# The last 128 output rows in 64-row product tiles, and a second program of products, evacuations and transfers appended to the kernel

## The chip, the core and the metric

The kernel runs on one core of a Trainium2 chip. The metric is device time in microseconds from the launch to the end of the program on that core; lower is better. One core has a matrix engine (PE, with its weight loads PEld), a vector engine (DVE), an activation engine (ACT), a general engine (POOL), a queue engine for transfers (SP) and 16 DMA engines. PE reads its operands from SBUF and writes to PSUM, which has 8 banks of 128 partitions by 512 float32.

## What is computed

A transformer layer with two parallel branches on a normalized input: attention with 32 query heads that share one key and one value head, and a two-layer network with squared ReLU.

```
xn = layernorm(x)                                  # x: 1 x 2048 x 640, bfloat16
q  = (xn @ wq) as 32 heads of 20;  k = xn @ wk;  v = xn @ wv
p  = softmax(q k^T * 20**-0.5) ;   o = p v
A  = o (heads joined, 640) @ wo
h  = relu(xn @ w1 + b1)**2                          # 1536 wide
B  = h @ w2 + b2
out = x + A + B                                     # 2048 x 640
```

## The kernel before

The sequence is cut into 4 column blocks of 512 queries and 16 tiles of 128 keys, and the 32 heads into 8 groups of 4, so that there are 32 blocks (query block, head group). For each block and key tile, PE makes the scores of four heads as four products that each use 20 to 32 rows of the array, one 32-row group per head (line 1014, and line 1231 for the other way below), ACT takes the exponential out of two or three PSUM banks at a time (line 1056), and PE multiplies by the values with four 32-column tiles of the array, one per head, into one bank, `PVB` (bank 7). A part of the score tiles goes another way: DVE writes an integer approximation of the exponential (line 1245), POOL makes further terms by integer additions (line 1265), and some terms are summed by accumulating transfers that POOL issues, 512 KB each (line 1280). The projections, the network and the output products run between the attention steps, again as four 32-column tiles per step (`col4`, line 426 is the one line that issues them, in `mm`).

No engine's order is written by hand. A planner in the kernel's own Python keeps a clock per engine, gives each operation a modelled duration, and repeatedly commits the operation that can start first; the order in which they were committed is the order in which each engine executes. [...]

**The end of the program.** The output of the last 512 rows is made in eight halves (`halves`: four row tiles, 12 to 15, of 128 rows, by two halves of 320 columns). Each half is a sum of six products: four blocks of attention output with `wo_c`, and two with `woe`, a padded copy of the last eight heads' rows of `wo` that is kept in the storage of `w1_sb` (so the profile calls it `w_sb`, and its left operand `QCr`). One product is four matmuls of 128 rows by 32 columns with 320 moving columns, one per 32 output rows. `tail_ops` (from line 1307) offers these products to the planner as banks come free, and `tail_done` (from line 1330) queues the evacuation of a finished half, a DVE addition of the network's part from `part` (line 1346), and after each second half the output transfer of that row tile (line 830, `odma`). The sixth product of every half needs the last head group's normalized output (`TB31`, a DVE transpose, line 1122). At the end SP waits for the output transfers' semaphores (line 1638).

Of the kernel before, what the change touches and what calls it, by code (L numbers as in the profile page):

```python
# [24 lines left out]
NCH = D // 128  # L25
NXR, NFP, NOS = 3, 4, 3
HW = D // 2
SCALE = DH ** -0.5
EPS = 1e-5
EXP_SHIFT = 50.0  # L30
# [14 lines left out]
XA = SCALE * LOG2E * 128.0  # L45
XB = (127.0 - EXP_SHIFT * LOG2E - math.log2(TNORM)) * 128.0

PTR = 16
NB = 7
# [155 lines left out]
def add(lst, fn, waits=(), inc=None, amt=1):  # L205
    wd = {}
    for c, v in waits:
        if v is None or v <= 0:
            continue
        key = id(c)  # L210
        if key not in wd or wd[key][1] < v:
            wd[key] = (c.sem, v)
    w = list(wd.values())
    tgt = None
    sem = None
    if inc is not None:
# [12 lines left out]

    lst.append(emit)  # L230
    return tgt


class Op:
    def __init__(self, name, eng, dur, parts, deps=(), lat=None, lock=False, mode="C", prio=3, dma=None):
        self.name, self.eng, self.dur, self.parts = name, eng, dur, parts
        self.deps = [d for d in deps if d is not None]
        self.lat, self.lock, self.mode, self.prio = lat, lock, mode, prio
        self.dma = dma
        self.start = self.fin = None  # L240
# [8 lines left out]
        self.dw = 0.0  # L249
        if dma is not None:  # L250
            dma.n += 16
            self.tgt = (dma, dma.n)
# [10 lines left out]
def bass_parallel_sum__grouped_kv_mqa__dense_activation_squared_relu__prompt_kernel(nc, A_x, A_wq, A_wk, A_wv, A_wo, B_x, B_w1, B_b1, B_w2, B_b2, out):  # L263
    es = ExitStack()
    with es:
# [3 lines left out]
        def newctr(name):  # L269
            return Ctr(es.enter_context(nc.semaphore(name)))  # L270
# [154 lines left out]
        def mm(out_, l, r, start, stop, tp):  # L425
            return lambda e: e.matmul(out_, l, r, start=start, stop=stop, tile_position=tp)  # L426
# [880 lines left out]
        def tail_ops():  # L1307

            r = []
            for x in halves:  # L1310
                if x["c"] < NCH:
                    bk = x["bank"] if x["bank"] is not None else tail_bank()
                    if bk is None:
                        break
                    t_ = tb_op.get((qe, x["c"]))
                    if t_ is None or t_.fin is None:
                        continue
                    r.append((x, bk, 2.5))
                    break
            for x in halves:  # L1320
                if x["c"] == NCH and (qe, NCH) in tb_op:
                    r.append((x, x["bank"], 1.9))
                    break
            for x, bk, p in r:
                c, st, h = x["c"], x["st"], x["h"]
                mats, cs = out_mats(st, h, [c], False)
                deps = [tb_op[(qe, c)]] + (l_woe[c - NCH + 1] if c >= NCH - 1 else l_wo) + ([bank_rel[bk]] if c == 0 else [])
                yield Op(f"OF{st}_{h}_{c}", "PE", 0.136, out_chunks(mats, bk, c == 0, c == NCH)[0][1](), deps), p, x, bk

        def tail_done(o, x, bk):  # L1330
            st, h = x["st"], x["h"]
            if x["c"] == 0:
                x["bank"] = bk
                bank_busy[bk] = True
            x["c"] += 1
            if x["c"] <= NCH:
                return
            cs = slice(h * HW, h * HW + HW)
            free_row = tn_op[NBLK - 1] if st == ST - 1 else dma_out.get(st - NOS)
            k = 2 * (st - 4 * qe) + h  # L1340
            if k in ACTEV:
                i = ACTEV.index(k)
                e_ = op(f"OFa{st}_{h}", "ACT", 0.40, lambda e: e.activation(out=xr[:, i, :], in_=ps[:, bk, 0:HW], func=AF.Identity), [o] + [fp_ev[n] for n in XORD[-NXR:]])
                f_ = op(f"OFe{st}_{h}", "POOL", 0.85, lambda e: e.tensor_tensor(out=orow(st)[:, cs], in0=xr[:, i, :], in1=part[:, st % 4, cs], op=ALU.add), [e_, fr_op[k], free_row])
            else:
                f_ = e_ = op(f"OFe{st}_{h}", "DVE", 0.40, lambda e: e.tensor_tensor(out=orow(st)[:, cs], in0=ps[:, bk, 0:HW], in1=part[:, st % 4, cs], op=ALU.add), [o, fr_op[k], free_row], prio=0.1)  # L1346
# [258 lines left out]

        for o in order_all:
            for d in o.deps:
                if not (o.eng == "PE" and d.eng == "PE"):
                    d.consumed = True

        clock = {k: {} for k in ENG}
# [1 line left out]
        for o in order_all:  # L1613
            ck = clock[o.eng]
            waits = []
            for d in o.deps:
                if o.eng == "PE" and d.eng == "PE":
                    continue
                c, v = d.tgt
                if ck.get(id(c), 0) >= v:  # L1620
                    continue
                waits.append((c, v))
                for i_, v_ in d.clock.items():
                    ck[i_] = max(ck.get(i_, 0), v_)
                ck[id(c)] = v
            o.clock = dict(ck)
            for k, fn in enumerate(o.parts):
                w = waits if k == 0 else ()
                if o.dma is not None:
                    add(lists[o.eng], lambda e, fn=fn, c=o.dma: fn(e).then_inc(c.sem, 16), waits=w)  # L1630
                elif k == len(o.parts) - 1 and o.consumed:
                    v = add(lists[o.eng], fn, waits=w, inc=eng_ctr[o.eng])
                    o.tgt = (eng_ctr[o.eng], v)
                    o.clock[id(eng_ctr[o.eng])] = v
                else:
                    add(lists[o.eng], fn, waits=w)
        for slot in range(NOS):
            add(lists["SP"], None, waits=[(osem[slot], osem[slot].n)])

# [54 lines left out]
```

## Time and profile before

| What | Value |
|---|---|
| Time, median of 2 runs | 676.42 us (675.42 to 677.43) |
| Span of the profiled execution | 688.3 us |
| Busy in that span: PE, DVE, ACT, POOL | 679.9, 607.2, 657.7, 586.2 us |
| Granted PE clock, mean | 0.973 of full speed |
| Last exponential (ACT) begins, ends | 678.29, 679.41 us |
| Last evacuation (DVE) ends | 686.1 us |
| Issue of the last output transfer | 686.12 us |

The profile shows one execution with the hardware profiler on. No device time of its own is recorded for that execution, only the span from its first to its last instruction; it is 11.9 us longer than the median of the two timed runs. Times in the views are counted from the start of the span. In the timeline, a row is a group of like instructions merged; its second number is the time from the start of its first to the end of its last. [...] The number in brackets is the idle time of the engine before the row, and who ended it.

### The profile page before, as it was taken

The page shows a single profiled execution, that of the slowest core. Times are in us where ns is not written, and L with a number is a line of the kernel's source. Part 1 is how long each engine was busy: PE and PEld are TensorE (multiplying, and loading weights), DVE is VectorE, ACT ScalarE, POOL GpSimd, SP SyncE. Part 2 cuts the span into 40 slices and gives each one's busy share as a digit, 9 for nine tenths or more (in the row PEclk, how much of TensorE's full clock was granted, in tenths as well). Part 3 has the DMA queues.
Part 4 walks back from the last instruction along what each step waited for, and adds up shares of the span by engine and source line. Part 5 has one row for each costly group of instructions (what it writes and reads, how often), then busy time and mean ns, then how long its engine had stood idle before and what let it go on. Part 6 is the DMA issues. An engine that isn't in the chain of part 4 may idle for free.

```text
span 688.3 us, 22356 instructions
## 1 busy us (share of the span) xinstructions
PE 679.9 (99%) x9554; PEld 212.3 (31%) x9555; DVE 607.2 (88%) x1081; ACT 657.7 (96%) x721; POOL 586.2 (85%) x597
## 2 busy tenths in 40 slices
PE   8999999999999999999999999999999999999998
PEld 4233222232322222333332222333332222233334
DVE  8558999899999899889998999889888999999893
ACT  6668999999999999999999999999999999999994
POOL 0406989889999999989999989999989998989982
PEclk9559999999999999999999999999999999999999
DMA  8355677767877697768977667677777765788873
GB/s 215 89 130 145 130 158 149 152 138 156 168 166 143 124 176 136 155 133 179 200 140 154 134 131 136 135 150 147 141 160 152 141 124 115 152 180 185 169 158 97
DMA packets 62894, 102.21 MB, mean 148 GB/s; under 512 B 22418, under 2 KB 40722, under 8 KB 62794
## 3 DMA queue, kind: packets, MB, share of 16 engines
q0 software_dynamic: 19296, 70.26, 54.8%
q1 hardware_dynamic: 41898, 30.14, 16.6%
q8 instruction: 75, 1.23, 0.7%
q10 hardware_dynamic: 1600, 0.38, 0.3%
q14 instruction: 25, 0.20, 0.1%
HBM read 17.71 MB, written 4.42 MB: 32 GB/s over the span
## 4 chain that ended last, share of the span: by engine, by line
PE 74%; ACT 15%; POOL 5%; DVE 3%; DMA 2%; issue 1%; DVEq 0%; POOLq 0%
PE ps L426 71%; ACT PT L1056 15%; POOL x_sb L1265 2%; DVE tmore L1245 2%; POOL tmore L1265 2%; PE ps L619 1%; DMA x_sb<-x_sb 1%; DMA tmore<-tmore 1%; PE ps L648 1%; POOL x_sb L1280 1%; DVE big L775 0%; DVE xr L823 0%; DVE out_sb L1346 0%; PE ps L581 0%; PE ps L576 0%
## 5 line engine op out<-in xcount | busy, mean ns | idle before, releaser
L1056 ACT ACTIVATE PT<-ps 128x1024 bf16<-128x1024 f32 (+2 forms) x697 | 644.7, 1107 | 16.1 <-PE ps L426 15.5
L1245 DVE TENSOR_SCALAR tmore<-ps 128x512 uint16<-128x512 f32 x644 | 417.9, 682 | 43.9 <-PE ps L426 37.9
L1265 POOL INT64_ADD tmore<-tmore x226 | 258.8, 1306 | 35.9 <-DVE tmore L1245 25.9
L426 PE MATMUL ps<-qT,kT 20*128 20x512 bf16 x2048 | 277.1, 390 | 1.2 <-ACT PT L1056 0.8
L1265 POOL INT64_ADD x_sb<-tmore x222 | 255.8, 1287 | 21.4 <-PE ps L426 4.7
L426 PEld LDWEIGHTS ps<-qT,kT 20*128 20x128 bf16 x2048 | 68.8, 91 | 265.0 <-ACT PT L1056 218.4
L426 PE MATMUL ps<-PT,vx 128*32 128x512 bf16 x1396 | 139.5, 395 | 0.1
L426 PE MATMUL ps<-xnT,w_sb 128*32 128x512 bf16 x960 | 79.3, 383 | 0.4 <-DVE tmore L1245 0.4
L426 PE MATMUL ps<-w_sb,big 128*32 128x320 bf16 x1536 | 79.2, 301 | 0.3
L1280 POOL DMA_DIRECT2D tmore<-tmore x65 | 71.2, 1112 | 2.5 <-POOL tmore L1265 2.4
L1280 POOL DMA_DIRECT2D x_sb<-tmore x65 | 67.7, 1048 | 4.8 <-POOL x_sb L1265 3.3
L426 PE MATMUL ps<-tmore,vxs 128*32 128x512 bf16 x640 | 58.3, 382 | 0.3 <-POOL tmore L1265 0.3
L426 PE MATMUL ps<-x_sb,vxs 128*32 128x512 bf16 x624 | 57.6, 383 | 0.2 <-DMA x_sb<-x_sb 0.2
L426 PEld LDWEIGHTS ps<-PT,vx 128*32 128x32 bf16 x1396 | 35.2, 93 | 73.1 <-issue 67.5
L426 PE MATMUL ps<-tmore,vx 128*32 128x512 bf16 x456 | 43.3, 382 | 0.4 <-DMA tmore<-tmore 0.4
L426 PEld LDWEIGHTS ps<-w_sb,big 128*32 128x32 bf16 x1536 | 34.3, 96 | 28.4 <-issue 16.8
L767 DVE TENSOR_SCALAR hT_tmp<-ps,b1col 128x512 bf16<-128x512 f32 x48 | 35.5, 740 | 0.9 <-PE ps L426 0.6
L426 PE MATMUL ps<-xnT,wq_sb 128*32 128x512 bf16 (+2 forms) x480 | 35.8, 366 | 0.2 <-ACT PT L1056 0.2
L426 PE MATMUL ps<-wo_c,OC 128*32 128x320 bf16 x608 | 31.6, 301 | 0.0
L426 PE MATMUL ps<-x_sb,vx 128*32 128x512 bf16 x320 | 31.3, 382 | 0.0
L775 DVE TENSOR_TENSOR big<-hT_tmp 128x512 bf16<-128x512 bf16 x48 | 28.2, 589 | 0.2
L426 PEld LDWEIGHTS ps<-xnT,w_sb 128*32 128x32 bf16 x960 | 19.8, 95 | 22.0 <-issue 15.4
(103 smaller groups left out, 324.5 us busy)
## 6 DMA issues: line engine op xcount, KB each, us to landing
x_sb<-tmore POOLq DMA_DIRECT2D x65, 512.0 KB, 5.4
tmore<-tmore POOLq DMA_DIRECT2D x65, 512.0 KB, 5.6
w_sb<-in_B_w_dram SPq DMA_DIRECT2D x8, 480.0 KB, 4.3
big<-OR SPq DMA_DIRECT2D x71, 40.0 KB
big<-drs SPq DMA_DIRECT2D x71, 40.0 KB
xh<-in_A_x_dram SPq DMA_DIRECT2D x32, 80.0 KB, 3.4
out_dram<-out_sb SPq DMA_DIRECT2D x15, 160.0 KB, 2.8
qT<-QCr SPq DMA_DIRECT2D x105, 20.0 KB
```

Source lines behind the costliest of these rows:

```text
L426: return lambda e: e.matmul(out_, l, r, start=start, stop=stop, tile_position=tp)
L619: return [lambda e: e.matmul(ps[:, PVB, :], ones_bf[:, :], hT_tmp[:, 0, :], start=True, stop=True)]
L648: return [(lambda e, dt=dt: e.transpose(out=psbf(bk)[:, dt * 128:(dt + 1) * 128], in_=xn_sb[:, st, dt * 128:(dt + 1) * 128], identity=iden ...
L767: o = Op(f"RL{qc}_{f}", "DVE", 0.66, [lambda e: e.tensor_scalar(out=hT_tmp[:, k % 2, :], in0=ps[:, bk, :], scalar1=b1col[:, f:f + 1], scal ...
L775: q = op(f"SQ{qc}_{f}", "DVE", 0.34, lambda e: e.tensor_tensor(out=h2T[:, f, :], in0=hT_tmp[:, k % 2, :], in1=hT_tmp[:, k % 2, :], op=ALU. ...
L1056: return Op(f"ACT{st_['j']}", "ACT", ACB + ACM * n, [lambda e: e.activation(out=to, in_=ps[:, b0:b0 + (n - 1) * db + 1:db, :], func=AF.Exp ...
L1245: d1 = op(f"D1_{n}_{i}", "DVE", 0.60, lambda e: e.tensor_scalar(out=L[:, cs].bitcast(U16), in0=ps[:, bank, :], scalar1=XA, scalar2=XB, op0 ...
L1265: fn = lambda e, T=T, j=j: e.int64_add(out=T.bitcast(I64), in0=L.bitcast(I64), in1=TSTEP * j * 0x0001000100010001)
L1280: p = op(f"AD{a}_{n}", "POOL", ADDUR, lambda e, src=src, dst=dst: e.dma_start(dst, src, accum_op=ALU.add), dp + [ad_last.get(k)], dma=adse ...
```

## The change

It has two parts.

**The last row tile.** `tail_ops` offers only the first six halves as before. When all six are complete, it offers the last two halves (row tile 15) as two PE operations named `OFX`, each of 48 matmuls of 64 rows by 32 columns (half the contraction each): the first takes rows 0 to 63 of column half 0 into one bank in turn with rows 64 to 127 of column half 1 into a second bank; the second takes the other row halves, accumulates into the same two banks, and waits by a semaphore for the completion of the first, although both are PE operations (`force`). The two banks are chosen among banks 0 to 6 by their planned release; in the built program these are bank 1 and bank 4, and bank 4 is released by the first evacuation of row tile 12. Up to the last product of the half 14/1, the built order of every engine is the same as before. Before, the first product of half 15/0 stood ahead of the six closing products, and half 15/1 went to bank 7.

**An appended program.** After the planner's lists are written out, further instructions are added whose results are not used. They begin when all eight evacuations are done (`wts`):

- PE: 617 matmuls with `vx` and `kT` as operands, each group of four covering the 32-column tiles: 8 groups with 128 rows; 24 groups with 64 rows, the two row halves in turn; 48 groups of such, with waits for a semaphore that PE itself raises; 9 groups, each of which waits for the group before; and six sets (4 groups of 128 rows; 8 groups all in rows 0 to 63; 16 groups of 320 columns in turn; 5 plain 128 by 128 products; 6 groups of 512 columns in turn with 6 of 320; 24 groups in turn over four banks), each of which waits for the set before.
- ACT: then 12 exponentials out of two or three banks (six of 1024 elements, six of 1536), each waiting for the one before.
- DVE: then 12 operations, each waiting for the one before: three of 512 and three of 1024 elements of the form of line 1245, two of 256 elements of the form of line 663, two float32 additions of 512, two operations with a scalar and a tensor of 512.
- POOL: then 6 accumulating transfers between parts of `tmore`, each waiting for the landing of the one before: 512 KB, 512 KB, 1 MB, 1 MB, 512 KB, 1 MB.
- SP waits for the last of these transfers before it waits for the output transfers.

```diff
         def tail_ops():
-            for x in halves:
+            for x in halves[:6]:
                 if x["c"] < NCH:
...
-            for x in halves:
+            for x in halves[:6]:
                 if x["c"] == NCH and (qe, NCH) in tb_op:
...
+            if all(x["c"] > NCH for x in halves[:6]) and halves[6]["c"] <= 0:
+                bs = sorted((bank_state(bk), bk) for bk in range(NB) if bank_state(bk) is not None)[:2]
+                second = halves[6]["c"] < 0
+                if len(bs) == 2 or second:
+                    b2 = [halves[6]["bank"], halves[7]["bank"]] if second else [bs[0][1], bs[1][1]]
+                    deps = [first_half[0]] if second else [tb_op[(qe, c)] for c in range(NCH + 1)] + l_woe[0] + l_woe[1] + l_wo + [bank_rel[bk] for bk in b2]
+                    parts = []
+                    for c in range(NCH + 1):
+                        for rg, h in ((0, 1), (1, 0)) if second else ((0, 0), (1, 1)):
+                            (l, r_), = out_mats(ST - 1, h, [c], False)[0]
+                            w = slice(64 * rg, 64 * rg + 64)
+                            for j in range(4):
+                                parts.append(mm(ps[32 * j:32 * j + 32, b2[h], 0:320], l[w, 32 * j:32 * j + 32], r_[w], c == 0 and not second, c == NCH and second, (64 * rg, 32 * j)))
+                    o = Op("OFX", "PE", 1.0, parts, deps)
+                    o.force = second
+                    yield o, 1.0, b2, None
...
+        wts = [fin_ev[k].tgt for k in fin_ev]
+        prs = newctr("prs")
+        def tl(rg, bk, n=512, wd=64, start=True):
+            p = slice(wd * rg, wd * rg + wd)
+            return [mm(ps[32 * j:32 * j + 32, bk, 0:n], vx[p, 0, :], kT[p, 0:n], start, True, (wd * rg, 32 * j)) for j in range(4)]
+        def put(fns, waits=(), mark=False):
+            for k, fn in enumerate(fns):
+                add(lists["PE"], fn, waits=waits if k == 0 else (), inc=prs if mark and k == len(fns) - 1 else None)
+            return [(prs, prs.n)]
+        p = []
+        for k in range(8):
+            p += tl(0, 0, 512, 128)
+        put(p, wts)
+        p = []
+        for k in range(12):
+            p += tl(0, 0) + tl(1, 1)
+        w = put(p, (), True)
+        for k in range(4):
+            w1 = put(tl(0, 0) + tl(1, 2) + tl(0, 0), w, True)
+            put(tl(1, 2) + tl(0, 3) + tl(1, 3 + 1))
+            w = put(tl(1, 0) + tl(0, 5) + tl(1, 0), w1, True)
+            put(tl(0, 5) + tl(1, 6) + tl(0, 1))
+        w = put(tl(0, 0), w, True)
+        for k in range(4):
+            w = put(tl(1, 0), w, True)
+            w = put(tl(0, 0), w, True)
+        gs = [[], [], [], [], [], []]
+        for k in range(4):
+            gs[0] += tl(0, 0, 512, 128)
+        for k in range(8):
+            gs[1] += tl(0, 1 + k % 2)
+        for k in range(8):
+            gs[2] += tl(0, 1, 320) + tl(1, 2, 320)
+        for k in range(5):
+            gs[3].append(mm(ps[:, 3, 0:512], xnT[:, 0, 0:128], kT[:, 0:512], True, True, (0, 0)))
+        for k in range(6):
+            gs[4] += tl(0, 4) + tl(1, 5, 320)
+        for k in range(6):
+            gs[5] += tl(0, 4) + tl(1, 5) + tl(0, 6) + tl(1, 7)
+        for p in gs:
+            w = put(p, w, True)
...
+        for bs in ((0, 2, 1), (0, 2, 1), (0, 3, 2), (0, 3, 2), (0, 4, 3), (0, 4, 3), (0, 3, 1), (0, 3, 1), (0, 5, 2), (0, 5, 2), (0, 7, 3), (0, 7, 3)):
+            n = len(range(*bs))
+            v = add(lists["ACT"], lambda e, bs=bs, n=n: e.activation(out=PT[:, 2:2 + n, :], in_=ps[:, bs[0]:bs[1]:bs[2], :], func=AF.Exp, bias=-EXP_SHIFT, scale=SCALE), waits=w + [(pa, v)], inc=pa)
...
+            v = add(lists["DVE"], fn, waits=wa + [(pd, v)], inc=pd)
+        wd = [(pd, v)] + wa
+        pg = newctr("prg")
+        for k, n in enumerate((1, 1, 2, 2, 1, 2)):
+            add(lists["POOL"], lambda e, n=n: e.dma_start(tmore[:, 1:1 + n, :], tmore[:, 4:4 + n, :], accum_op=ALU.add, max_dma_last_dim=4096).then_inc(pg.sem, 16), waits=wd + [(pg, 16 * k)])
+        add(lists["SP"], None, waits=[(pg, 96)])
         for slot in range(NOS):
             add(lists["SP"], None, waits=[(osem[slot], osem[slot].n)])
```

More of the change, by code (lines that the diff above doesn't have):

```diff
@@ L1616, in bass_parallel_sum__grouped_kv_mqa__dense_activation_squared_relu__prompt_kernel @@
             for d in o.deps:
-                if o.eng == "PE" and d.eng == "PE":
+                if o.eng == "PE" and d.eng == "PE" and not o.force:
                     continue
@@ new lines, in bass_parallel_sum__grouped_kv_mqa__dense_activation_squared_relu__prompt_kernel @@
+        wa = [(pa, v)] + w
+        v = 0
+        for k in range(12):
+            if k < 3:
+                fn = lambda e: e.tensor_scalar(out=tmore[:, 0, 0:512].bitcast(U16), in0=ps[:, 0, :], scalar1=XA, scalar2=XB, op0=ALU.mult, op1=ALU.add)
+            elif k < 6:
+                fn = lambda e: e.tensor_scalar(out=tmore[:, 0, 0:1024].bitcast(U16).rearrange("p (a n) -> p a n", a=2), in0=ps[:, 0:2, :], scalar1=XA, scalar2=XB, op0=ALU.mult, op1=ALU.add)
+            elif k < 8:
+                fn = lambda e: e.tensor_scalar(out=kT[:, 0:256], in0=ps[:, 2, 0:256], scalar1=nk0[:, 1:2], scalar2=nhalf[:, 0:1], op0=ALU.add, op1=ALU.mult)
+            elif k < 10:
+                fn = lambda e: e.tensor_tensor(out=OR[:, 2, :], in0=ps[:, 3, :], in1=OR[:, 2, :], op=ALU.add)
+            else:
+                fn = lambda e: e.scalar_tensor_tensor(out=PT[:, 6, :], in0=ps[:, 3, :], scalar=b1col[:, 0:1], in1=PT[:, 7, :], op0=ALU.add, op1=ALU.mult)
+            v = add(lists["DVE"], fn, waits=wa + [(pd, v)], inc=pd)
```

19 lines of the change are left out of this document (18 added, 1 removed).

## The prediction

> **What bounds the kernel now.** I read the page for the engines' shares and the chain, then the timeline of the last 35 us, then the groups by form for prices, the transfers around the last accumulating transfer, and the stretches with the granted clock. Page, span and chain:
>
> ```profile
> span 688.3 us, 22356 instructions
> ...
> PE 679.9 (99%) x9554; PEld 212.3 (31%) x9555; DVE 607.2 (88%) x1081; ACT 657.7 (96%) x721; POOL 586.2 (85%) x597
> ...
> PE 74%; ACT 15%; POOL 5%; DVE 3%; DMA 2%; issue 1%; DVEq 0%; POOLq 0%
> ```
>
> PE and ACT bound the body, but the built order of all engines is the same up to the last product of half 14/1, so the body costs nothing either way. Only the end matters. Timeline:
>
> ```profile
> 659.23 0.39 PE L426 MATMUL ps<-qT,kT 20*128 20x512 bf16 x3
> ...
> 682.45 1.00 PE L426 MATMUL ps<-w_sb,QCr 128*32 128x320 bf16 x24
> 682.82 2.48 DVE L1346 TENSOR_TENSOR out_sb<-ps,w_sb 128x320 bf16<-128x320 f32 x6 [0.43 <-PE ps L426]
> ...
> 684.49 0.44 PE L426 MATMUL ps<-w_sb,QCr 128*32 128x320 bf16 x8
> 685.22 0.88 DVE L1346 TENSOR_TENSOR PT<-ps,w_sb 128x320 bf16<-128x320 f32 x2
> 686.12 0.33 SPq L830 DMA_DIRECT2D out_dram<-PT  x1
> ```
>
> See three things. The first row has three products in three row groups finished in 0.39 us, the length of one: row groups work side by side. In the second, 24 matmuls, six groups of four column tiles, take 1.00 us with a last record of 0.30: a group of 320 columns every 0.136 us (the same count gives 0.216 us at 512 columns). And DVE, not PE, sets the end: its eight evacuations run without a gap until 686.10, and PE is through at 684.93. Prices, groups by form:
>
> ```profile
> L1056 ACT ACTIVATE PT<-ps 128x1024 bf16<-128x1024 f32 x671 | 623.4, 1107 | 14.3 <-PE ps L426 13.8
> L1245 DVE TENSOR_SCALAR tmore<-ps 128x512 uint16<-128x512 f32 x644 | 417.9, 682 | 43.9 <-PE ps L426 37.9
> L426 PE MATMUL ps<-PT,vx 128*32 128x512 bf16 x1396 | 139.5, 395 | 0.1
> L767 DVE TENSOR_SCALAR hT_tmp<-ps,b1col 128x512 bf16<-128x512 f32 x48 | 35.5, 740 | 0.9 <-PE ps L426 0.6
> L1056 ACT ACTIVATE PT<-ps 128x1536 bf16<-128x1536 f32 x14 | 20.3, 1502 | 1.7 <-PE ps L426 1.7
> L663 DVE TENSOR_SCALAR kT<-ps,nk 128x256 bf16<-128x256 f32 x6 | 2.9, 484 | 11.0 <-PE ps L426 10.9
> ```
>
> The last accumulating transfer of the program, issued at 673.23 (stretch 672.5 to 679):
>
> ```profile
> DMA  0004000000000939393929293939369920000000
> ...
> q0 software_dynamic: 160, 0.52, 42.6%
> ...
> tmore<-tmore POOLq DMA_DIRECT2D x1, 512.0 KB, 4.5
> ```
>
> It is alone: 4.5 us from issue to landing, and the DMA engines show eight rounds of about 0.34 us. In the body the page gives 5.4 to 5.6, with others in flight. The clock, by stretches (PE busy first, clock third from the end):
>
> ```profile
> 13.68:17.10 3.42, 2.58 (x51) 1.20 (x50) 2.57 (x8) 2.40 (x3) 0.00 (x0) 1.00 1.05 210
> 17.10:20.50 3.40, 3.40 (x29) 0.85 (x25) 2.12 (x8) 2.62 (x3) 1.75 (x3) 0.50 0.49 142
> ...
> 58.06:61.47 3.41, 3.27 (x57) 1.40 (x49) 2.61 (x6) 3.41 (x4) 2.62 (x3) 1.00 0.12 28
> 682.70:686.10 3.40, 2.24 (x68) 1.49 (x56) 3.27 (x8) 0.00 (x0) 0.00 (x0) 1.00 0.24 83
> ```
>
> The clock's changes in the trace (6.86, 17.10, 54.64, 689.52) are whole multiples of 3.413 us apart. Counted by cadence instead of records, PE was filled 0.41 in the stretch before the fall at 17.10, and 0.60 and 0.61 in the last two rows, after which the clock held. It rose again after a stretch filled 0.89, not after one of 0.86.
>
> **The change part by part.** All sums are against the profiled execution: span 688.3, no own time beside it, 11.9 above the median of the timed runs. I add the difference to 676.42.
>
> *Last row tile.* Two banks are needed, and one is released by the first evacuation (682.82 + 0.49 = 683.31); DVE to PE takes 0.054 in the trace, so the first 48 products start at 683.37, not 683.28. With the row halves side by side they are six rounds of 0.136: the last record ends at 684.34; after the wait (PE to PE is not in the trace; DVE to PE 0.054 stands for it, 0.2 bounds it from above, 0 from below) the second six end at 685.38. Behind that wait only the appended products queue. DVE is free at 685.22 but must now wait until 685.45, and its last evacuation ends at 686.33: +0.23. The six evacuations before it hid PE, and that cover is gone.
>
> *Appended products*, from 686.38. Rounds of 512 columns: 8 + 12 + 24 in the first three parts, 35 in the sets (4, 8, 5, 6, 12), 79 x 0.216 = 17.1; eight rounds of 320, 1.1. Nine links that wait for themselves: record 0.395 + 0.054, nine times, 4.1. Eight other waits each cost a record less a cadence plus 0.054, 0.23: 1.8 at most, and the waits inside the third part are covered by the three groups between. Sum 24.1, to 710.5.
>
> *ACT.* A 1024-element exponential alone takes 1.02 (the mean 1.107 has others in its way; the shortest record is 1.017); 1536 adds 0.43, the step from the 512 form (0.591) to it. An engine's wait for itself is 0.03 in the trace (DVE 48 times, ACT once). 6 x 1.05 + 6 x 1.48 = 15.2; the means give 16.0.
>
> *DVE.* 512 elements 0.68; 1024 from the slope between 320 (0.480) and 512 (0.682), 1.22; 256 as the 484 ns row, 0.49; float32 additions 0.68; scalar and tensor between 0.68 and the 740 ns row, 0.71. With 0.03 each: 2.1 + 3.8 + 1.0 + 1.4 + 1.5 = 9.8 (9.3 to 10.6).
>
> *Transfers.* 512 KB alone: 4.55. 1 MB is not in the trace. From below, eight more rounds and nothing else, 7.25; from above, two single ones, 9.1; the issue (0.86) may double as well, so I take half of that, 7.7, nearer the lower end because rounds are what the row shows. From landing to the next issue, POOL's waits lie between 0.02 (DVE after a landing) and 0.30 (POOL before an issue): 0.15. 0.1 + 3 x 4.55 + 3 x 7.7 + 5 x 0.15 = 37.6; bounds 35.5 and 45.1 (5.4 each and 9.1). [...]
>
> *Sum.* 710.5 + 0.04 + 15.2 + 0.03 + 9.8 + 37.6 = 773.2; 0.4 from the landing to the end of the span, as at 687.9. 773.6 - 688.3 = 85.3, so 676.42 + 85.3 = 761.7, **762**. The last output transfer lands beneath it. If prices shrink with the ratio of the timed to the profiled execution (0.983), 1.5 less.
>
> **The rivals.**
>
> *The clock halves in the nine links.* They fill 0.216 of every 0.449, 0.48 for 4.1 us: between the 0.41 that fell and the 0.60 that held. A window must lie mostly within them, and the sets behind fill 0.8 to 0.9, about the bound for rising. Two windows at half speed lose up to 3.4 us: 765. [...]
>
> *Row halves follow one another.* For: no row of before has 64-row tiles of 32 columns. Against: the three row groups in 0.39, and column tiles side by side everywhere. Price: 12 x 0.136 in the last tile, 12 + 24 + 12 rounds of 0.216, and 14 of 0.136 in the sets: 1.6 + 10.4 + 1.9 = 13.9, or 776.
>
> *Transfers without the fixed part.* If a transfer alone cost only its eight or sixteen rounds, 3 x 2.7 + 3 x 5.4 + 0.9 = 25.2, the kernel is at 749. The 4.5 stands against it.
>
> *Not slower.* The appended work would have to run beside the body, its place being idle time of POOL (102 us), DVE (81) and ACT (31); the first product would have to be released long before the evacuations. It decides from 71.8 of the 85.3 us hidden, and then gives 676 to 690. [...]
>
> **How the numbers follow.** The forecast 0.50, the halved clock 0.33, row halves in sequence 0.11, cheap transfers 0.03, not slower 0.01, something else 0.02. The forecast's own range is 758 (lower bounds, or the smaller prices of a timed run) to 769 (transfers near their upper bound). With the clock's 3 us and part of the sequential case, 757 to 774 holds 8 in 10. About 2% is what a measurement of this kernel can tell from no change; slower by more has 0.98, within 0.01, faster 0.01.
>
> **What would show it.** Eight 64-row products within one record, and 0.216 us per pair of groups; DVE's last evacuation near 686.3 instead of 686.1; ACT's first appended exponential about 24 us later; 15 us of ACT, 10 of DVE; issue to landing 4.5 and 7.7. It is wrong if two groups of opposite row halves start 0.2 us apart, if the clock row falls below 1 within the products, or if 1 MB lands after more than 8.5 us.

## The result and the profile after

The kernel with the change takes 771.3 us (771.1 and 771.5) against 676.42 before: a ratio of 1.141 (95% interval 1.136 to 1.145), 94.9 us more. The forecast was 762, so it has the direction and nine tenths of the size; 9.6 us (94.9 less 85.3) are missing from its sum. The profiled execution of the kernel after has a span of 769.4 us and an own time of 771.5.

One thing has to be known before the two profiles are compared. The profiled execution of before ran at half clock from 17.1 to 54.6 us, inside the body, and is 12 us longer than the timed ones (single executions that are 8 to 17 us longer at a lower mean clock occur below too, and the ratios leave them out); that of after has no such stretch, so the two spans can't be subtracted. I count instead from two landmarks that both have: the last transpose that DVE copies into QCr (682.39 us before, 671.17 after), and the end of the last evacuation (686.09 before, 675.22 after).

The page of the kernel after:

```profile
span 769.4 us, 23751 instructions
...
PE 688.1 (89%) x10220; PEld 219.0 (28%) x10220; DVE 615.5 (80%) x1093; ACT 671.3 (87%) x733; POOL 592.5 (77%) x603
...
PEclk9999999999999999999999999999999999998555
...
PE 55%; ACT 14%; POOL 10%; DMA 10%; DVE 6%; issue 3%; SPq 0%; POOLq 0%; ACTq 0%
```

Before, the chain of waits gave DMA 2%; now DMA has 10%, and the clock row ends in fives (0.50 from 704.50 us on); the last slices have no products. The timeline around the last row tile and the first appended products:

```profile
671.59 2.48 DVE L1379 TENSOR_TENSOR out_sb<-ps,w_sb 128x320 bf16<-128x320 f32 x6 [0.43 <-PE ps L427]
672.15 0.74 PE L427 MATMUL ps<-wo_c,OC 64*32 64x320 bf16 x32
672.70 0.46 PE L427 MATMUL ps<-w_sb,QCr 64*32 64x320 bf16 x16
673.25 0.74 PE L427 MATMUL ps<-wo_c,OC 64*32 64x320 bf16 x32
673.80 0.46 PE L427 MATMUL ps<-w_sb,QCr 64*32 64x320 bf16 x16
674.33 0.89 DVE L1379 TENSOR_TENSOR PT<-ps,w_sb 128x320 bf16<-128x320 f32 x2 [0.26 <-PE ps L427]
675.25 0.33 SPq L831 DMA_DIRECT2D out_dram<-PT  x1
675.27 18.79 PE L427 MATMUL ps<-kT,vx 128*32 128x512 bf16 x468 [1.02 <-DVE PT L1379]
```

Two things can be seen. Thirty-two 64-row products, four rounds of eight tiles, start at 672.15 and the next sixteen at 672.70: 0.14 us a round, as for one group of 128 rows before, so row halves do run side by side. And DVE, which had no gap before, now waits 0.26 us for PE ahead of the last two evacuations. The second half of the 48 products starts 1.10 us after the first.

The timeline of the appended work on the other engines:

```profile
699.91 15.87 ACT L1718 ACTIVATE PT<-ps 128x1024 bf16<-128x1024 f32 x12 [31.73 <-PE ps L427]
715.80 2.34 DVE L1723 TENSOR_SCALAR tmore<-ps 128x512 uint16<-128x512 f32 x3 [40.59 <-ACT PT L1718]
718.28 3.94 DVE L1725 TENSOR_SCALAR tmore<-ps 128x1024 uint16<-128x1024 f32 x3
722.37 1.23 DVE L1727 TENSOR_SCALAR kT<-ps,nk,nhalf 128x256 bf16<-128x256 f32 x2
723.72 1.52 DVE L1729 TENSOR_TENSOR OR<-ps,OR 128x512 f32<-128x512 f32 x2
725.38 1.64 DVE L1731 SCALAR_TENSOR_TENSOR PT<-ps,b1col,PT 128x512 bf16<-128x512 f32 x2
727.33 0.87 POOL L1736 DMA_DIRECT2D tmore<-tmore  x1 [63.37 <-DVE PT L1731]
732.44 0.86 POOL L1736 DMA_DIRECT2D tmore<-tmore  x1 [4.24 <-DMA tmore<-tmore]
737.58 1.22 POOL L1736 DMA_DIRECT2D tmore<-tmore  x1 [4.28 <-DMA tmore<-tmore]
746.10 1.19 POOL L1736 DMA_DIRECT2D tmore<-tmore  x1 [7.30 <-DMA tmore<-tmore]
754.64 0.88 POOL L1736 DMA_DIRECT2D tmore<-tmore  x1 [7.35 <-DMA tmore<-tmore]
759.77 1.20 POOL L1736 DMA_DIRECT2D tmore<-tmore  x1 [4.25 <-DMA tmore<-tmore]
```

Nothing overlaps: each engine starts when the one before it has ended, as the listed waits say. In the transfers of this stretch (size, then issue to landing) the two sizes stand apart:

```profile
DMA  0499006990049999900399999006980069999800
...
tmore<-tmore POOLq DMA_DIRECT2D x3, 1024.0 KB, 8.0
tmore<-tmore POOLq DMA_DIRECT2D x3, 512.0 KB, 4.6
```

The zeros are time in which no DMA engine moves anything: after each landing POOL needs 0.56 us to the next issue, and then 1.43 to 1.79 us pass to the first packet.

### The profile page after: what moved, and what is told of

Its sections match the earlier page's. It is cut to its first block, busy times and chain, and to the rows that moved or that the text cites. A ratio compares the mean times of both kernels' runs of the same rounds, so it can differ in the third digit from the quotient of the medians.

```text
span 769.4 us, 23751 instructions
## 1 busy us (share of the span) xinstructions
PE 688.1 (89%) x10220; PEld 219.0 (28%) x10220; DVE 615.5 (80%) x1093; ACT 671.3 (87%) x733; POOL 592.5 (77%) x603
## 4 chain that ended last, share of the span: by engine, by line
PE 55%; ACT 14%; POOL 10%; DMA 10%; DVE 6%; issue 3%; SPq 0%; POOLq 0%; ACTq 0%
PE ps L427 55%; ACT PT L1057 12%; DMA tmore<-tmore 6%; POOL x_sb L1266 4%; POOL tmore L1266 4%; DVE tmore L1246 2%; ACT PT L1718 2%; DMA x_sb<-tmore 2%; POOL x_sb L1281 1%; DMA xnT<-big 1%; DVE OR L518 1%; DMA x_sb<-in_A_x_dram 1%; POOL tmore L1281 1%; DMA R<-drs 1%; DVE big L776 0%
## 5 line engine op out<-in xcount | busy, mean ns | idle before, releaser
L427 PE MATMUL ps<-qT,kT 20*128 20x512 bf16 x2048 | 271.9, 384 | 1.6 <-ACT PT L1057 0.8
L427 PE MATMUL ps<-PT,vx 128*32 128x512 bf16 x1396 | 137.3, 388 | 0.1
L1736 POOL DMA_DIRECT2D tmore<-tmore x6 | 6.2, 1038 | 90.8 <-DVE PT L1731 63.4
L1281 POOL DMA_DIRECT2D tmore<-tmore x65 | 70.9, 1106 | 2.5 <-POOL tmore L1266 2.4
L1718 ACT ACTIVATE PT<-ps 128x1024 bf16<-128x1024 f32 (+1 forms) x12 | 14.9, 1238 | 32.7 <-PE ps L427 31.7
```

The lines of the kernel that those rows point to most:

```text
L1281: p = op(f"AD{a}_{n}", "POOL", ADDUR, lambda e, src=src, dst=dst: e.dma_start(dst, src, accum_op=ALU.add), dp + [ad_last.get(k)], dma=adse ...
L1718: v = add(lists["ACT"], lambda e, bs=bs, n=n: e.activation(out=PT[:, 2:2 + n, :], in_=ps[:, bs[0]:bs[1]:bs[2], :], func=AF.Exp, bias=-EXP_ ...
L1736: add(lists["POOL"], lambda e, n=n: e.dma_start(tmore[:, 1:1 + n, :], tmore[:, 4:4 + n, :], accum_op=ALU.add, max_dma_last_dim=4096).then_ ...
```

## The experiments

Eleven kernels ran, in three groups, each beside runs of the kernel before on the same chip (medians 675.94, 675.17 and 674.61 us).

**The last row tile alone.** The appended block is taken out; the new order of the last tile stays.

```
-        wts = [fin_ev[k].tgt for k in fin_ev]
-        ...
-        add(lists["SP"], None, waits=[(pg, 96)])
```

> The changed last row tile alone, nothing appended. Theory A (all of the change's time lies in the appended parts, and the last tile costs only the 0.35 us that DVE waits in the changed profile): 676.4 + 0.35 = 676.8 us, within the interval of the kernel before. Theory B (the last tile in 64-row products costs some 2.5 us beyond what the profile shows at the end, since the sum of the appended parts leaves 2.5 us of the 94.9 unexplained): 679 us.

Measured: 677.38 us, ratio 1.0019 (1.0006 to 1.0033), 1.3 us more (0.4 to 2.2). From the last transpose to the last evacuation it is 4.05 us instead of 3.70, the 0.35 that the first theory asks for; the 2.5 of the other does not occur. A second 0.35 us lies behind the evacuation, in the timeline:

```profile
671.53 2.75 SPq L831 DMA_DIRECT2D out_dram<-out_sb  x3
...
673.35 0.89 DVE L1379 TENSOR_TENSOR PT<-ps,w_sb 128x320 bf16<-128x320 f32 x2 [0.26 <-PE ps L427]
...
674.33 0.43 SPq L831 DMA_DIRECT2D out_dram<-PT  x1
```

The three output transfers ahead hold SP's queue until 674.28: the third of them took 1.16 us to issue here instead of 0.43, and the last one goes out 0.09 us after the evacuation has ended instead of 0.03, and its own issue is 0.43 instead of 0.33: 0.16 of the second 0.35. The rest of the 1.3 us can't be told from the spread of the executions.

**The appended work alone.** The kernel before with the appended block at its end.

> The last row tile as before, all appended parts. Theory A (the time is in the appended parts; the last tile costs 0.36 in the profile up to the last evacuation and up to 1.3 in the timed runs of the tile alone): 770.0 to 771.0 us, against 771.3 for the whole change. Rival (the last tile's row halves are worth or cost more when products follow directly behind): outside 769 to 772.

Measured: 772.73 us, ratio 1.1437 (1.1410 to 1.1464). From the last transpose to the last evacuation 3.70 us, as before. So the old tile saves 0.35 us in the trace and nothing that the times show. The median is over the 770.0 to 771.0 that were expected, and by its wording the rival (outside 769 to 772) is right; but the trace of the appended part is the same (94.16 us from the last evacuation to the end, 94.15 with the new tile), and the two groups of times account for the rest. The seven times fall into two groups: 767.83 and 768.74 with a mean clock of 0.958, and five of 772.45 to 774.67 with 0.950 to 0.953. The first group is the one of the profiled execution, in which the clock did not fall in the products.

**The products alone.** The block is cut behind the last product.

> The changed last tile and the appended PE products; the appended exponentials, DVE operations and transfers are left out. Theory A (parts stand one behind the other and nothing else changes): 676.4 + 0.35 for the tile + 24.6 for the products + 0.6 to the end of the program - 2.2 for the old end, which lies beneath = 699.8 us. Theory B (a program with an appended part pays 2.5 us elsewhere, in the body): 771.3 less the 69.0 us from the last product to the end in the changed profile = 702.3 us.

Measured: 701.73 us, ratio 1.0382 (1.0344 to 1.0419), but no execution stands near that median: 698.19 and 699.48 at a mean clock of 1.0, 703.98 and 704.19 at 0.993. The profiled execution is of the second kind; its products took 29.1 us, with the clock at 0.5 from 686.8 to 697.0. Theory A's 699.8 fits the first two within 1.6 us, and neither theory fits the other two. The prediction's rival that halves the clock is therefore right in some executions and wrong in others of one and the same program. The three experiments on links below look for what decides it.

**Transfers beside the products.** POOL's transfers wait for the last evacuation instead of for DVE's last appended operation.

```
-  max_dma_last_dim=4096).then_inc(pg.sem, 16), waits=wd + [(pg, 16 * k)])
+  max_dma_last_dim=4096).then_inc(pg.sem, 16), waits=[(pg, 16 * k)] if k else wts)
```

> The six appended transfers start when the eight evacuations are done, beside the appended products, exponentials and DVE operations, instead of behind them. Theory A (they cost 40.7 us only because they stand last, and 1.4 us more because the program ends right behind them, in POOL's closing drain): the end follows the last DVE operation, 52 us after the evacuations, so 771.3 - 41.8 = 729.5 us. Rival (transfers and products disturb each other in SBUF, or the closing cost stays): 731 us or more.

Measured: 734.67 us, ratio 1.0868 (1.0842 to 1.0895): 36 us less than the whole change, so the transfers stand on the path that sets the end. But 729.5 is missed by 5, and the rival's 731 or more holds: products and transfers disturb each other. Products take 32.3 us instead of 24.6, and the transfers are slower (5.2 to 5.7 us for 512 KB, 9.2 and 9.6 for two of the 1 MB). It is the products that count, since the last transfer has landed 15.2 us before the end. The end gets cheaper: 0.28 us from DVE's last operation to the end of the span, not 1.67 behind the last landing. The timeline has a new kind of line, a product that waited for nothing the profile shows:

```profile
681.33 3.99 PE L427 MATMUL ps<-kT,vx 64*32 64x512 bf16 x128 [0.70 <-issue]
...
685.37 1.22 POOL L1736 DMA_DIRECT2D tmore<-tmore  x1 [4.60 <-DMA tmore<-tmore]
...
686.99 1.28 PE L427 MATMUL ps<-kT,vx 64*32 64x512 bf16 x18 [1.67 <-issue]
```

Here the clock fell too (0.5 from 691.1 to 701.3), behind these two standstills and a window that lies in the nine links.

**One wait instead of several.** Each appended operation of ACT, DVE and POOL waits only for the one before it; the first of each still waits for the engine before. The longer lists of the change are redundant.

```
-  scale=SCALE), waits=w + [(pa, v)], inc=pa)
+  scale=SCALE), waits=[(pa, v)] if v else w, inc=pa)
...
-  v = add(lists["DVE"], fn, waits=wa + [(pd, v)], inc=pd)
+  v = add(lists["DVE"], fn, waits=[(pd, v)] if v else [wa[0]], inc=pd)
...
-  max_dma_last_dim=4096).then_inc(pg.sem, 16), waits=wd + [(pg, 16 * k)])
+  max_dma_last_dim=4096).then_inc(pg.sem, 16), waits=[(pg, 16 * k)] if k else [wd[0]])
```

> Each link of the appended ACT, DVE and POOL chains waits for one semaphore, its own, instead of two to four, of which the others have long been reached; the order and the work are the same. Theory A (the links that were mis-sized are the extra wait instructions: in the changed profile 0.09 on ACT, 0.14 on DVE, 0.56 on POOL, against 0.03, 0.03 and 0.1 to 0.3): 11 x 0.06 + 11 x 0.10 + 5 x 0.3 to 0.45 + 0.2 ahead of the first transfer = 3.5 to 4.2 us less, 767.1 to 767.8 us. Rival (a link is the semaphore's own way to the engine, whatever the number of waits): 771.3 us.

Measured: 768.78 us, ratio 1.1379 (1.1355 to 1.1404), an interval that overlaps that of the whole change. The profiled execution's clock fell in the products (27.7 us), so the total hides what the parts show:

```profile
699.69 15.19 ACT L1718 ACTIVATE PT<-ps 128x1024 bf16<-128x1024 f32 x12 [34.87 <-PE ps L427]
714.91 2.14 DVE L1723 TENSOR_SCALAR tmore<-ps 128x512 uint16<-128x512 f32 x3 [43.06 <-ACT PT L1718]
717.09 3.74 DVE L1725 TENSOR_SCALAR tmore<-ps 128x1024 uint16<-128x1024 f32 x3
...
723.47 1.54 DVE L1731 SCALAR_TENSOR_TENSOR PT<-ps,b1col,PT 128x512 bf16<-128x512 f32 x2
725.30 0.87 POOL L1736 DMA_DIRECT2D tmore<-tmore  x1 [64.72 <-DVE PT L1731]
```

ACT's twelve operations take 15.19 us instead of 15.87, DVE's twelve 10.10 instead of 11.22, and POOL's five links 0.28 to 0.29 us each instead of 0.56. That is 3.2 us for waits that were already over, where 3.5 to 4.2 was expected. With one wait, a link costs 0.03 on ACT and DVE, the value that the prediction took from the body. The number of waits is not all of it: DVE's first appended operation lists two waits in the whole change and one here, POOL's first transfer three and one, and both start as soon in either (0.03 us behind ACT, 0.30 behind DVE), so the 0.2 expected ahead of the first transfer did not occur. In the trace of the whole change, further waits are instructions of their own ahead of the operation. In the links the wait that ends last stands on such an instruction; for these first operations it stands on the operation itself. That this place is what costs is read from the traces, and no run changed it alone.

**The whole change again**, unaltered, beside the experiments of its group.

> The changed kernel itself, again, for its spread beside the others on the same chip. Theory A (the clock falls in the nine links in some executions, by where the windows of 3.413 us lie, and costs about 3 us then): single times between 769 and 776, in two groups 3 to 4 us apart. Rival (the clock does not differ between executions and the body alone varies): a spread of 3 us or less, as the kernel before has outside its disturbed runs.

Measured: 770.3 us, ratio 1.1396 (1.1364 to 1.1427). Of its six times three, 767.83 to 769.07, go with a mean clock of 0.956 to 0.958, and two, 771.53 and 772.89, with 0.953 and 0.952; the sixth is 786.74 us at 0.928. Among the five there are two groups some 3.7 us apart, as expected, but a microsecond or more lower. Its profiled execution had no fall in the products: 24.6 us.

**Twenty-five links instead of nine.** One number in the loop of products that wait for themselves, `range(4)`, becomes `range(12)`.

> 25 links that wait for themselves instead of 9, the rest of the changed kernel the same. Full speed: 16 more links at 0.455 = 7.3 us, 778.6 us, products 31.9 us long. Theory A (the clock is judged in windows of 3.413 us by how much of a window PE streams; in three runs so far it fell after windows filled 0.46, 0.47 and 0.53 and held after 0.57): some whole windows lie in the links at 0.47, so the clock falls in every run, the later links take about 0.66 and the sets run at half speed until a window filled over 0.87: products 35 to 40 us, 782 to 787 us. [...]

Measured (one execution): 783.74 us; products 39.9 us. The stretches, cut at the clock's own steps (PE busy first, clock third from the end):

```profile
680.57:683.98 3.41, 3.19 (x88) 0.99 (x72) 0.00 (x0) 0.00 (x0) 0.00 (x0) 1.00 0.02 5
683.98:687.40 3.42, 2.92 (x32) 0.69 (x28) 0.00 (x0) 0.00 (x0) 0.00 (x0) 1.00 0.00 0
687.40:690.81 3.41, 3.06 (x24) 0.54 (x20) 0.00 (x0) 0.00 (x0) 0.00 (x0) 0.50 0.00 0
```

The time and the fall are those of theory A. In the second line PE's records fill 2.92 of 3.42 us, no idle gap is over 0.07 us, and the clock falls at the line's end: no idle window stands ahead of this fall. Besides the time that PE streams, how much of the array the products fill is left as a candidate.

**Twenty-five links with 128 rows.** The same chain of links, the same 512 columns, but each link's four tiles are 128x32 and fill the whole array.

```
-        w = put(tl(0, 0), w, True)
-        for k in range(4):
-            w = put(tl(1, 0), w, True)
-            w = put(tl(0, 0), w, True)
+        w = put(tl(0, 0, 512, 128), w, True)
+        for k in range(12):
+            w = put(tl(0, 0, 512, 128), w, True)
+            w = put(tl(0, 0, 512, 128), w, True)
```

> 25 links that wait for themselves as before, but each product has 128 rows instead of 64; columns, cadence and waits are the same, so PE streams for the same 0.47 of a window but fills the whole height of the array. Theory C (the clock falls by the share of the array that is filled over a window of 3.413 us: counted with rows and columns, every fall so far followed a window of 0.33 or less and every window of 0.34 or more held; the 64-row links are 0.22, these 0.47): no fall, products 32 us long, 768 + 7.3 = 775 us. Rival A (the clock goes by streamed time alone, 0.47 is below what fell): a fall as with 64 rows, products 40 us, 783 us.

Measured (one execution): 777.74 us, 2.7 more than expected; products 32.2 us as expected, and no fall in them. Stretches inside its links:

```profile
685.00:688.40 3.40, 2.86 (x32) 0.72 (x28) 0.00 (x0) 0.00 (x0) 0.00 (x0) 1.00 0.00 0
688.40:691.80 3.40, 2.85 (x32) 0.77 (x32) 0.00 (x0) 0.00 (x0) 0.00 (x0) 1.00 0.00 0
691.80:695.20 3.40, 2.89 (x32) 0.77 (x32) 0.00 (x0) 0.00 (x0) 0.00 (x0) 1.00 0.00 0
```

Same number of records and nearly the same busy time as the 64-row links, in a row of windows, and the clock holds. Four 64x32 tiles are half the array: a link about every 0.47 us that streams for 0.216 (the cadence of 512 columns) fills, by an estimate from these two numbers, 0.46 of the array's time with 128 rows and 0.23 with 64. It is one execution of each.

**Nine links on both row halves.** Each of the nine links gets the other row half as well (eight tiles, two banks), nothing else changes in length.

```
-        w = put(tl(0, 0), w, True)
-        for k in range(4):
-            w = put(tl(1, 0), w, True)
-            w = put(tl(0, 0), w, True)
+        for k in range(9):
+            w = put(tl(0, 3) + tl(1, 2), w, True)
```

> The nine links carry both row halves side by side on two banks, twice the work in each link, otherwise the changed kernel. Theory C (share of the array filled): no window under 0.34 among the products, so the clock does not fall in them; the links cost 9 x 0.02 more; products 24.6 to 24.8 us in every execution, single times 767.5 to 771.5 us, median 768.5 to 769.5, none near 773. Rival A (streamed time alone): single times up to 773 as with the changed kernel, median 770 to 772.

Measured: 769.63 us (768.11 to 770.58), ratio 1.1396 (1.1378 to 1.1413). All five executions have a mean clock of 0.955 to 0.957, and the profiled one has no fall in the products (24.9 us, where 24.6 to 24.8 was expected). Twice the work in the links, and the group of times near 773 does not occur again, as the theory of the array's share asks; the median is 0.1 us above its range and 0.4 below that of the rival. Of the other four executions only the mean clock is known, and the one at 0.955 lies just under the 0.956 to 0.958 of executions without a fall. What separates the two theories is the clock in the traces of 25 links: the same streamed time, with a fall at 64 rows and none at 128.

**Transfers beside products, links on both halves.** The two edits together, to see whether the standstills come from the clock.

> Links with both row halves, and the transfers beside the products as in the earlier run, where PE stood still twice for 2.4 us waiting for nothing that the profile shows, and the clock fell twice. Theory D (the standstills come with the transfers, for example since PE's instructions arrive over the same DMA engines): products 26 to 28 us without a fall of the clock, 730 to 732 us. Rival (they came with the clock's fall): products 24.8 us, 728.5 us.

Measured: 732.49 us, ratio 1.0855 (1.0825 to 1.0884); products 30.2 us with a fall of the clock, where 26 to 28 without one was expected, and 730 to 732 in all. PE's waits in the products, from the view of waits (us in all, number, longest):

```profile
PE ps L427 <- issue: 2.2, 2, 1.4
```

And its stretches:

```profile
679.00:683.00 4.00, 3.17 (x104) 1.28 (x98) 0.00 (x0) 0.00 (x0) 0.86 (x1) 1.00 0.48 93
683.00:687.00 4.00, 2.60 (x94) 0.92 (x86) 0.00 (x0) 0.00 (x0) 1.22 (x1) 1.00 0.25 46
687.00:691.00 4.00, 3.53 (x58) 0.70 (x44) 0.00 (x0) 0.00 (x0) 0.00 (x0) 0.65 1.08 191
```

The standstills (0.82 us up to 681.46, 1.40 up to 686.85) stand in the first and second lines, where the clock is 1.00; the fall is in the third, and lasts from 688.2 to 695.0. So the standstills come ahead of the fall, and they come with the transfers: the products of the whole change and of the nine links on both halves have none. The second one empties the window before the fall (array share 0.32), which fits a fall brought about by it. Why PE stands still was not settled. In both runs with transfers beside products each standstill ends 1.3 to 1.6 us after a transfer of instructions has landed (at 685.28 us for the second one here). Those two transfers start 5.0 and 10.3 us after the first product; with no transfers beside them the first two start after 3.0 and 6.3 us (nine links on both halves). That fits instruction words that are held up by the data, but no run took that cause away by itself.

**Row halves apart.** In the last tile the loop over the row half goes outside the loop over the chunks, and the second appended part does the twelve groups of one row half ahead of those of the other.

```
-                    for c in range(NCH + 1):
-                        for rg, h in ((0, 1), (1, 0)) if second else ((0, 0), (1, 1)):
+                    for rg, h in ((0, 1), (1, 0)) if second else ((0, 0), (1, 1)):
+                        for c in range(NCH + 1):
...
-        for k in range(12):
-            p += tl(0, 0) + tl(1, 1)
+        for rg in range(2):
+            for k in range(12):
+                p += tl(rg, rg)
```

> The same 64-row products in another order: in the last tile all lower row halves of one column half come before the upper ones of the other, and in the 24 appended groups the 12 of rows 0 to 63 come before the 12 of rows 64 to 127; no row half in turn. Theory A (two row halves run side by side when they are neighbours in the order): each half operation of the last tile takes 11 to 12 rounds of 0.136 instead of 6, the last evacuation ends 1.3 us later after the last transpose (5.3 instead of 4.05 us), and the 24 groups take 23 to 24 rounds of 0.216, 2.4 us more: 775.0 us. Rival (the order does not matter, since the queue ahead finds the other row half): 771.3 us and 4.05 us.

Measured (one execution): 775.36 us. That it is near 775.0 is chance: products took 30.9 us, with a fall of the clock from 688.8 us among them. From the last transpose to the last evacuation 4.58 us, 0.53 more than with the halves in turn, where 1.3 more was expected. The 24 appended groups lie ahead of the fall, at full clock, and can be compared by their weight loads (timeline rows). With the halves in turn, in the whole change:

```profile
677.11 2.29 PEld L427 LDWEIGHTS ps<-kT,vx 64*32 64x32 bf16 x96 [0.42 <-issue]
```

With the halves apart:

```profile
674.59 4.03 PEld L427 LDWEIGHTS ps<-kT,vx 64*32 64x32 bf16 x96 [0.42 <-issue]
```

That is 1.74 us more, eight rounds of 0.216, where 2.4 was expected: of the twelve groups of each half, four run beside four of the other and eight run alone. The timeline of the tile shows where the two halves meet:

```profile
669.09 0.75 PE L427 MATMUL ps<-wo_c,OC 64*32 64x320 bf16 x24
669.64 0.31 PE L427 MATMUL ps<-w_sb,QCr 64*32 64x320 bf16 x4
669.67 0.31 PE L427 MATMUL ps<-wo_c,OC 64*32 64x320 bf16 x4
...
671.80 0.89 DVE L1379 TENSOR_TENSOR PT<-ps,w_sb 128x320 bf16<-128x320 f32 x2 [0.79 <-PE ps L427]
```

Four products of one half and four of the other start 0.03 us apart although the program has them one after the other. DVE waits 0.79 us instead of 0.26. Direction as expected, size two fifths in the tile and seven tenths in the 24 groups: neighbours in the order run side by side, and some four groups at the seam do so as well, so neither theory is right as a whole.

## Why the prediction was right, and where it was 9.6 us short

The mechanism is as forecast: nothing of the appended work is hidden, and its stages follow each other. From the end of the last evacuation to the end of the span the trace has 94.15 us; the prediction's sum had 87.3. The 771.3 us lie inside the 757 to 774 that were to hold 8 in 10, but outside the 758 to 769 of the sum itself. What takes them in is the allowance for the clock and for row halves in sequence, and the profiled execution (771.5 us) had neither: that the wide range holds there is luck. By terms:

| term | predicted | measured | |
| --- | --- | --- | --- |
| last tile, to the last evacuation | +0.23 | +0.35 | |
| appended products | 24.1 | 24.57 | when the clock holds; a link 0.449, measured 0.47 |
| ACT, 12 operations with links | 15.2 | 15.87 | links 0.03, measured 0.09 |
| DVE, 12 operations with links | 9.8 | 11.22 | links 0.03, measured 0.14 |
| DVE to POOL | 0.1 | 0.30 | |
| three transfers of 512 KB | 13.65 | 13.7 | 4.56 to 4.57 each |
| three transfers of 1 MB | 23.1 | 23.9 | 7.93 to 7.97 each |
| five links between transfers | 0.75 | 2.8 | 0.15, measured 0.56 |
| last landing to the end | 0.4 | 1.67 | |

- **Last tile.** The reasoning held step by step: row halves side by side, two operations 1.10 us apart (predicted 1.04), DVE waiting for the last of them. The rounds take 0.136 us but for the first of each half (0.146), the eighth tile of a round starts 0.024 us after the first, and PE's wait for itself takes 0.09 and not 0.054 us.
- **Products.** When the clock holds, the cadence was right and the links were 0.02 us each too cheap. "The clock halves in the nine links" was given as a rival with 0.33 and 3 us. It is no alternative: the same program does both, and where the clock falls, the prediction is wrong by its own sign ("if the clock row falls below 1 within the products"). By the mean clock it fell in three of seven executions of the whole change and in five of seven with the old tile, and these are on average 2.5 and 4.9 us longer than the others of their kernel. The bound by which I judged it, the share of time that PE streams, did not hold: 25 links that stream for the same time fell with 64 rows and held with 128. The 9 links were between "the 0.41 that fell and the 0.60 that held", but by the share of the array they are at 0.22, and every fall counted here follows 0.338 or less. In the trace of the whole change, without a fall among the products, the 3.413 us windows begin at 684.02 and 687.43 us and have 0.54 and 0.40; one from 685.68 would lie wholly in the links. That this position decides which executions fall is my reading.
- **ACT and DVE.** The operations were priced right, within 0.03 us in all on ACT (1024 elements 1.024, 1536 1.451), and within 0.3 us in all on DVE (256 elements with two scalars per partition 0.545 instead of 0.49, scalar and tensor 0.751 instead of 0.71). The failed step is "an engine's wait for itself is 0.03": the rows behind it have one wait, and these operations list two (ACT) and three (DVE). Waits that are long over can still cost: 0.06 us a link on ACT, 0.10 on DVE. The experiment with one wait shows it.
- **Transfers.** 512 KB was right to 0.02 us. For 1 MB the choice between 7.25 and 9.1 came out at 7.96: the first packet comes 0.34 us later, since the issue takes 1.20 us instead of 0.87 (I took 0.43), and the eight more rounds take the other 3.06 instead of 2.7. The failed step is the link, "0.15" between 0.02 and 0.30: it is 0.56 with four waits listed, 0.285 with one. With one wait, the row of 0.30, POOL before an issue, was the right one, and it was diluted with a row of another engine.
- **The end.** "0.4 from the landing to the end of the span, as at 687.9" took the price of a transfer on SP's queue. Behind a transfer that POOL issued, POOL goes on until 769.14, and the span ends 1.67 us after the landing. With the transfers out of the way earlier it ends 0.28 us after the last work. With the transfers beside the products POOL also goes on for 1.44 us behind the last landing, but there DVE's work ends later still. That POOL's closing is the cause is read from the traces; no run changed it alone.
- **The remainder.** 94.15 less the 2.21 that before has behind its last evacuation is 91.9; with 0.35 of the tile, 92.3 of the 94.9. The other 2.6 fits the body: undisturbed profiles have the last transpose between 667.5 and 671.2 us whatever follows it, and after's was at the upper end (671.17). That is chance, and no term of the sum. In the other timed execution (771.1 us) the clock fell, by its mean of 0.951; I did not separate the two.
- **The rivals.** Row halves in sequence: excluded by the first timeline. Transfers without a fixed part: excluded, 1.43 to 1.79 us pass from issue to first packet. Not slower: excluded, the time is 94.9 us longer and each stage waits for the one before.

## What to carry to other kernels

Price a chain of dependent operations by a row that lists the same waits in the same places, not by the shortest link in the trace: operations that listed two to four waits, all but one over long before, lost 3.2 us over 27 links, while the first ones of DVE and POOL listed two and three and lost nothing. A time that falls into two groups need not be noise (here some 3.6 us apart in the whole change again, at mean clocks of 0.956 to 0.958 and 0.952 to 0.953): look at the mean clock of each execution, and where it differs, ask how full the array was in the emptiest stretch of 3.4 us (here 0.338 or less ahead of every fall, by the count below). And when work is moved beside other work, charge both sides: transfers moved under the products gave 36 us instead of the 41.8 expected, because the products beside them took 7.7 us longer.

## What the runs showed of the hardware that was not expected

- **What stands ahead of the clock's falls.** In all traces of this case I weighted each product by the share of the 128x128 array that its tile covers (20 rows or columns count as 32), for 0.216 us per 512 columns, twice that at half clock (256 columns every 0.213 in before's stretch from 17.10), and counted in windows of 3.413 us from the clock's first change: its changes before (6.86, 17.10, 54.64, 689.52) and after (4.77, 704.50) are whole multiples of that apart. The shares are estimates by this count. Every window before a fall then has 0.338 or less, 0.22 to 0.33 for those among the products, and every window at full clock after which it held has 0.350 or more (0.39 is the least in the whole change). Time streamed does not separate them (0.42 fell at 17.10 in before, 0.39 held at 11.60 in the whole change), idle gaps do not either (the clock held after one of 1.73 us that ended at 10.74 in the whole change, and fell with none over 0.07 in 25 links). Before's fall at 17.10 follows a window of 0.32 and fits. All this rests on that count: with 20 counted as 20, a window that held (from 15.01 in the whole change) has only 0.32. When the clock rises again I could not find: it rose after windows of 0.72 and more (0.89 in before), and not after some of 0.64 to 0.78.
- **Waits that are over can cost time.** A link cost 0.03 us with one wait and 0.09 with two on ACT, 0.03 with one and 0.14 with three on DVE, 0.285 with one and 0.56 with four on POOL ahead of a transfer. The first operations of DVE and POOL, with two and three waits, lost nothing.
- **Products beside accumulating transfers stand still** for 0.7 to 1.7 us at a time with no wait in the profile, and the transfers of 512 KB take 5.0 to 5.7 instead of 4.56 us. The cause is open.
- **Groups in different row halves start 0.02 to 0.03 us apart** (671.15 and 671.17, 669.64 and 669.67 with the halves apart) even where the program's order has them one after the other, for some four groups at the point where the halves meet.
